# Decode attention over a 1 GB cache: K in 64 KiB rows, one loop per engine, V slots freed by the last product, the gate computed at the start

## The chip, the cores and the metric

One core of one Trainium2 chip runs the kernel alone. The metric is device time in microseconds (us). Each kernel also left one profiled execution, whose span is 1.8 to 2.4 us below its time. Engines: PE does matrix products, DVE is the vector engine, ACT the scalar engine, SP issues DMAs; POOL does almost nothing here (1.4 us busy before). SBUF is the on-chip memory, PSUM the memory into which PE writes. PE's granted clock is the share of its full speed that the profile shows.

## The reference

One query token, 16 heads of 256, a cache of 65536 keys per head, all bf16. The attention output is multiplied by a gate.

```python
xn = _layernorm(x)
q = (xn @ wq).reshape(B, Sq, H, Dh).transpose(0, 2, 1, 3)      # H=16, Dh=256
scores = einsum("bhqd,bhkd->bhqk", q, k_cache) * Dh ** -0.5    # 65536 keys a head
o = einsum("bhqk,bhkd->bhqd", softmax(scores), v_cache)
s = o.transpose(0, 2, 1, 3).reshape(B, Sq, H * Dh) @ wo
g = silu(silu(xn @ w1) @ w2)                                   # the gate
return x + s * g
```

K and V are 537 MB each and are read once. Weights are 10.6 MB.

## The kernel before

A block is 16384 keys: 128 partitions of 128 keys, 8 MiB of K and 8 MiB of V; there are 64. Each block is cut in two tiles of 64 keys per partition, so a partition's row of a tile is 32 KiB. DVE multiplies 13 of every 32 keys by the query in one large product, which ACT sums key by key, and does the other 19 with a fused multiply and sum. Then the block's maximum goes DVE, PE, DVE, PE; ACT takes the exponential; PE multiplies by V one block later.

```python
KT = 64; SUB = 32; ND = 19; TPB = 2
...
    def sp_block(i):                        # K of block i, V of block i - 1, tile by tile
        for t in range(TPB):
            take(sp, kf[t])                 # wait until DVE has freed this K slot
            sp.dma_start(out=Kt[t][:, :], in_=src(Kd, i, t)).then_inc(kl[t], 16)
            take(sp, vf[t])                 # wait until PE has freed this V slot
            sp.dma_start(out=Vt[t][:, :], in_=src(Vd, i - 1, t)).then_inc(vl[t], 16)
...
    def pe_turn():                          # transposes the block's output O
        take(pe, oc)
        ...
                if a == 0 and j == 0:
                    ins.then_inc(vf[1], 1)  # the second V slot is freed here
...
        with nc.Fori(1, NBLK - 1, 1, engines={ET.PE, ET.DVE, ET.Activation, ET.SP}, ...) as i:
            sp_block(i)
            dve_block(i)                    # the query is in SBUF for all heads (qb)
            act_block(i)
            act_keep(i - 1)
            pe_bcast()
            pe_attend()
            pe_rows()
            pe_turn()
```

Block 0 stands ahead of the loop as straight code, the last block behind it. The gate's inner product is done at the start; its last activation is done in the tail.

## Time and profile before

| | before |
|---|---|
| time, median of the first three runs | 2529.64 us (2527.97 to 2530.91) |
| profiled span | 2527.2 us |
| last input packet ends | 2519.7 us |
| tail after it | 7.5 us |
| block period in the middle | 38.87 us |

Two more views matter for what follows. The first gives three stretches after the start. Its columns are the stretch and its length, the busy time and number of instructions of PE, of PE's weight loads, of DVE, ACT and POOL, then PE's granted clock, the busy share of the DMA engines and GB/s:

```profile
60.00:76.00 16.00, 8.61 (x32) 2.96 (x32) 16.00 (x75) 10.20 (x52) 0.00 (x0) 0.87 1.03 442
76.00:84.00 8.00, 3.85 (x10) 1.18 (x11) 8.00 (x40) 4.92 (x25) 0.00 (x0) 0.50 0.98 419
84.00:100.00 16.00, 7.16 (x34) 3.17 (x33) 13.85 (x66) 8.93 (x43) 0.00 (x0) 0.71 0.99 428
```

The DMA share stays at about 1: the start leaves no hole. The second is the end of the chain that ended last (start, duration, what):

```profile
2507.89 3.54 PE ps_a L308 x16
2511.43 1.03 PE ps_t L343 x8
2512.46 3.54 PE ps_a L308 x16
2516.00 1.51 PE ps_ao L679 x8
2517.52 1.03 PE ps_t L343 x8
2518.55 4.64 PE ps_ao L679 x24
```

PE works without a break from the last V products through the projection. The tail is PE's, while the stream is DMA's.

### The profile page before, as it was taken

What the parts mean: (1) busy time and instruction counts of PE and PEld (TensorE: products, weight loads), DVE (VectorE), ACT (ScalarE), POOL (GpSimd) and SP (SyncE); (2) the same over time, 40 slices, a digit from 0 to 9 for tenths busy, and PEclk for the clock granted to TensorE, in tenths of its full rate; (3) what the DMA queues carried; (4) which work ended last, traced back from release to release, by engine and by line L of the source; (5) the groups of instructions that cost most, each with busy time, mean ns of one, the idle gap of its engine ahead of it and who ended that gap; (6) DMA issues with size and microseconds to landing.
All of it is one profiled execution on the core that took longest, in us unless ns stands there. A gap on an engine that the chain in (4) does not pass through costs nothing. (4 is left out here: it accounts for less than half of the span.)

```text
span 2527.2 us, 30558 instructions
## 1 busy us (share of the span) xinstructions
PE 1284.5 (51%) x4945; PEld 483.4 (19%) x4945; DVE 2219.2 (88%) x10276; ACT 1446.6 (57%) x6996; POOL 1.4 (0%) x12
## 2 busy tenths in 40 slices
PE   3554455455544554555455445544554455445547
PEld 1111121111111211111112111111121111111212
DVE  7989898898898988988989889889898898898886
ACT  5656565655565656555656565556565655565553
POOL 0000000000000000000000000000000000000000
PEclk7777777777777777777767776777677767776778
DMA  9999999999999999999999999999999999999998
GB/s 413 432 432 432 432 432 432 432 432 432 432 432 433 432 433 432 432 432 432 432 432 432 432 432 432 432 432 432 432 432 432 432 432 433 432 432 432 432 432 346
DMA packets 40450, 1084.46 MB, mean 429 GB/s; under 512 B 4338, under 2 KB 6516, under 8 KB 6644
## 3 DMA queue, kind: packets, MB, share of 16 engines
q1 hardware_dynamic: 40434, 1084.31, 99.8%
q8 instruction: 4, 0.07, 0.0%
q14 instruction: 10, 0.08, 0.0%
q10 hardware_dynamic: 2, 0.00, 0.0%
HBM read 1084.29 MB, written 0.00 MB: 429 GB/s over the span
## 5 line engine op out<-in xcount | busy, mean ns | idle before, releaser
L262 ACT ACTIVATE junk_a<-prod 128x256 bf16<-128x256 bf16 x3328 | 1330.7, 401 | 746.9 <-ACTq L141 746.9
L308 PE MATMUL psO<-V,PV 128*2 128x512 bf16 x4064 | 1165.2, 458 | 1097.6 <-PEq L141 1097.6
L226 DVE CUSTOM_DVE_ANT_0 junk_d<-K,qcur 128x256 bf16<-128x256 bf16 x4864 | 1698.7, 414 | 0.0
L308 PEld LDWEIGHTS psO<-V,PV 128*2 128x2 bf16 x4064 | 388.4, 97 | 1847.6 <-issue 1520.3
L212 DVE TENSOR_TENSOR prod<-K,qcur 128x3328 bf16<-128x3328 bf16 x256 | 482.9, 1886 | 247.0 <-DVEq L141 247.0
L262 ACT ACTIVATION_READ_ACCUMULATOR junk_a<-prod 128x1 f32 x3328 | 620.0, 186 | 0.0
L226 DVE DVE_READ_ACCUMULATOR2_ANT S<- 128x1 f32 x4864 | 374.2, 77 | 0.0
L295 ACT COPY O<-psO 2x512 f32<-2x512 f32 x64 | 36.8, 574 | 202.4 <-ACTq L141 202.4
L343 PE MATMUL ps_t<-eye,O 2*128 2x1 f32 x520 | 69.6, 251 | 48.4 <-PEq L141 48.4
L343 PEld LDWEIGHTS ps_t<-eye,O 2*128 2x128 f32 x520 | 65.9, 192 | 69.0 <-issue 68.9
L297 ACT COPY hist<-ps_t 128x2 f32 (+1 forms) x65 | 10.4, 160 | 94.9 <-ACTq L141 94.9
L301 PE MATMUL ps_nb<-gmax,ones_row 1*128 1x1 bf16 x65 | 10.3, 159 | 56.1 <-PEq L141 55.6
L191 DVE COPY qcur<-qb 128x256 bf16 (+1 forms) x64 | 14.5, 227 | 25.4 <-issue 15.8
L284 ACT ACTIVATE PV<-S,hist 128x128 bf16<-128x128 f32 (+1 forms) x65 | 26.0, 400 | 2.1
L199 DVE COPY S<-S 128x128 f32<-128x128 f32 (+1 forms) x65 | 14.7, 226 | 9.5
L200 DVE TENSOR_REDUCE rmax<-S 128x1 bf16<-128x128 f32 (+1 forms) x65 | 18.2, 280 | 0.2 <-issue 0.2
L180 DVE TENSOR_REDUCE gmax<-ps_m 1x1 bf16<-1x128 f32 x65 | 17.8, 274 | 0.5 <-DVEq L141 0.5
L301 PEld LDWEIGHTS ps_nb<-gmax,ones_row 1*128 1x128 bf16 x65 | 6.0, 92 | 60.8 <-issue 60.5
L333 PE MATMUL ps_m<-ident,rmax 128*1 128x128 bf16 x65 | 14.3, 220 | 5.7 <-PEq L141 5.7
L488 PE MATMUL ps_a<-xnT,V 128*64 128x1 bf16 x112 | 6.7, 256 | 18.2 <-DMA V<-in_B_w_dram 18.2
L284 ACT ACTIVATION_READ_ACCUMULATOR PV<-S,hist (+1 forms) x65 | 12.1, 186 | 0.0
L488 PEld LDWEIGHTS ps_a<-xnT,V 128*64 128x64 bf16 x112 | 6.6, 210 | 18.7 <-DMA V<-in_B_w_dram 18.7
(65 smaller groups left out, 79.3 us busy)
## 6 DMA issues: line engine op xcount, KB each, us to landing
K<-in_A_k_cache_dram SPq DMA_DIRECT2D x126, 4096.0 KB, 21.3
V<-in_A_v_cache_dram SPq DMA_DIRECT2D x125, 4096.0 KB, 28.7
K<-in_A_k_cache_dram SPq DMA_DIRECT2D x4, 2048.0 KB, 18.5
V<-in_A_v_cache_dram SPq DMA_DIRECT2D x4, 2048.0 KB, 22.9
W<-in_A_v_cache_dram SPq DMA_DIRECT2D x2, 2048.0 KB, 27.3
W<-in_A_wq_dram SPq DMA_DIRECT2D x1, 3072.0 KB, 10.4
K<-in_A_wo_dram SPq DMA_DIRECT2D x3, 896.0 KB, 31.4
V<-in_B_w_dram SPq DMA_DIRECT2D x1, 1568.0 KB, 35.5
```

The lines of the kernel that those rows point to most:

```text
L180: dve.reduce_max(out=gmax[0:1, :], in_=ps_m[0:1, :], axis=AX.X).then_inc(gm, 1)
L191: q_t = own(dve.tensor_copy(out=qcur[:, :], in_=qb[:, sub(q0, Dh)]))
L199: dve.tensor_copy(out=S2[:, c0:c1], in_=S[:, c0:c1]).then_inc(f, 1)
L200: dve.reduce_max(out=rmax[:, :], in_=S[:, c0:c1], axis=AX.X).then_inc(rm, 1)
L212: m = dve.tensor_tensor(out=prod[k % 2][:, :, :], in0=Kv[:, s * SUB + ND : (s + 1) * SUB, :], in1=qcur[:, None, :].to_broadcast([P, NA, Dh ...
L226: ins = dve.tensor_tensor_reduce(out=junk_d[jk][:, :], in0=Kv[:, s * SUB + j, :], in1=qcur[:, :], scale=1.0, scalar=0.0, op0=ALU.mult, op1 ...
L262: ins = act.activation(out=junk_a[jk][:, :], in_=prod[k % 2][:, j, :], func=ACT.Identity, accum_out=S[:, a : a + 1],)
L284: act.activation(out=PV[:, c0:c1], in_=S2[:, c0:c1], func=ACT.Exp, bias=neg, scale=scale, accum_out=hist[:, at(i), 1:2].rearrange("p o s - ...
L295: act.copy(out=O[:, :], in_=po[:, :]).then_inc(oc, 1)
L301: pe.matmul(ps_nb[:, 0:1], lhsT=ones_row[0:1, :], rhs=gmax[0:1, :], start=True, stop=True).then_inc(bm, 1)
L308: ins = pe.matmul(po[:, :], lhsT=PV[:, c0 + c : c0 + c + 2], rhs=T[:, (k0 + c) * Dh : (k0 + c + 2) * Dh], start=(start and c == 0), stop=( ...
L343: ins = pe.matmul(ps_t[:, a : a + 1], lhsT=Ov[:, j, a, :], rhs=eye2[:, j : j + 1], start=(j == 0), stop=(j == 1),)
```

## The change

The intent: fewer, longer DMA packets on a DMA-bound kernel (432 or 433 GB/s in every slice but the first and the last), with the buffers that this needs. K comes in whole blocks of 64 KiB per partition in two 8 MiB slots; V stays in halves of 32 KiB. To make room, the scratch tiles go (DVE and ACT write their throw-away outputs in place), one product tile instead of two, and the weights live in the V slots at first. The query of the next block comes from PE through PSUM. Each engine has its own loop. The gate is finished before the loops and stays in PSUM. The last pieces are ordered anew. Core of the diff, with cuts:

```diff
+    Kt = [pool.tile([P, KB * Dh], bf16, name=f"K{t}") for t in range(2)]   # KB = 128: 64 KiB rows
+    def load_k(i, s):
+        take(sp, kf[s])
+        sp.dma_start(out=Kt[s][:, :], in_=block(Kd, i)).then_inc(kl[s], 16)
...
+    def pe_block(i):
+        take(pe, pv)
+        for t in range(2):
+            take(pe, vl[t], 16)
+            pe_keys(psO, Vt[t], 0, PV, t * VT, VT, t == 0, t == 1, vf[0] if t == 0 else od)
+        pe.matmul(
+            ps_z, lhsT=ident[:, 0:1], rhs=ident[:, 0:1], start=True, stop=True
+        ).then_inc(vf[1], 1)          # second V slot freed right after the products
+        pe_rows(); pe_turn(); pe_bcast()
+        pe_query(i + 1)
...
+        load_rows(wq_t, A_wq, HD, dl["wq"])
+        load_rows(w12_t, B_w1, F, dl["w12"])          # w1, w2 now ahead of K
+        ...
+        for s in range(2):
+            sp.dma_start(out=Kt[s][:, :], in_=block(Kd, s)).then_inc(kl[s], 16)
+        with loop(ET.SP, 0, NBLK - 4, 2) as i:
+            for s in range(2):
+                load_v(i + s)
+                load_k(i + s + 2, s)
...
+        load_keys(Vt[1], VT, Vn, VT, VT + VT // 2, vl[1])        # next-to-last V
+        load_keys(Vt[1], VT, Vn, VT + VT // 2, KB, v2)
+        load_keys(Kt[1], 0, Kl, VT, KB, kh)                      # second half of the last K
...
+        t_g = silu(ps_y, ps_y, prod[...], t)          # the whole gate, before DVE's loop
+        with loop(ET.DVE, 0, NBLK - 2, 2, hint_back_edge=True) as i:
+            for s in range(2):
+                dve_block(s)
+        with loop(ET.Activation, 0, LAST, 1) as i:
+            act_block(i)
```

## The prediction

> **What bounds the kernel now.** I read the page first: busy shares, then the slices, then the queue.
>
> ```profile
> PE 1284.5 (51%) x4945; PEld 483.4 (19%) x4945; DVE 2219.2 (88%) x10276; ACT 1446.6 (57%) x6996; POOL 1.4 (0%) x12
> ...
> DMA  9999999999999999999999999999999999999998
> GB/s 413 432 432 432 432 432 432 432 432 432 432 432 433 432 433 432 432 432 432 432 432 432 432 432 432 432 432 432 432 432 432 432 432 433 432 432 432 432 432 346
> DMA packets 40450, 1084.46 MB, mean 429 GB/s; under 512 B 4338, under 2 KB 6516, under 8 KB 6644
> ...
> q1 hardware_dynamic: 40434, 1084.31, 99.8%
> ```
>
> The reader is to see a flat 432 GB/s from the second slice to the last but one, with all 16 DMA engines busy; only the two ends are lower. No compute engine is full. So the time is start + bytes / rate + tail. Grouped by size, the trace's DMA packet records say the same: 16 packets are in flight in nearly all of 100 to 2400 us, the first data packet starts at 2.02 us and the last input packet ends at 2519.7 us. The tail after it is 2527.2 - 2519.7 = 7.5 us. The timed median, 2529.64, is 2.4 us above the profiled span.
>
> The runner-up is DVE, so I read its waits and one stretch of its timeline in the middle:
>
> ```profile
> DVE prod L212 <- DVEq L141: 247.0, 124, 2.6
> ```
>
> ```profile
> 1215.16 0.23 DVE L199 COPY S<-S 128x128 f32<-128x128 f32 x1
> 1215.31 0.28 DVE L200 TENSOR_REDUCE rmax<-S 128x1 bf16<-128x128 f32 x1
> 1215.84 0.23 DVE L191 COPY qcur<-qb 128x256 bf16 x1 [0.25 <-issue]
> 1217.51 1.89 DVE L212 TENSOR_TENSOR prod<-K,qcur 128x3328 bf16<-128x3328 bf16 x1 [1.44 <-DVEq L141]
> 1237.05 1.89 DVE L212 TENSOR_TENSOR prod<-K,qcur 128x3328 bf16<-128x3328 bf16 x1 [2.53 <-DVEq L141]
> 1245.43 1.89 DVE L212 TENSOR_TENSOR prod<-K,qcur 128x3328 bf16<-128x3328 bf16 x1
> ```
>
> DVE waits twice a block before the big product, 1.44 and 2.53 us here, for K to land: some 4 us of slack in each block. The block period is 38.87 us (K issues at 1215.63 and 2420.47 are 31 blocks apart). The last two rows give a step (product plus 19 fused sums) that nothing delays: 1245.43 - 1237.05 = 8.38 us.
>
> Last, the tail:
>
> ```profile
> 2496.07 0.20 DVE L199 COPY S<-S 128x64 f32<-128x64 f32 x1
> 2496.18 0.21 DVE L200 TENSOR_REDUCE rmax<-S 128x1 bf16<-128x64 f32 x1
> 2496.54 0.22 PE L333 MATMUL ps_m<-ident,rmax 128*1 128x128 bf16 x1 [0.27 <-PEq L141]
> 2496.91 0.28 DVE L180 TENSOR_REDUCE gmax<-ps_m 1x1 bf16<-1x128 f32 x1 [0.51 <-DVEq L141]
> 2497.33 0.16 PE L301 MATMUL ps_nb<-gmax,ones_row 1*128 1x1 bf16 x1 [0.57 <-PEq L141]
> 2523.22 0.61 DVE L688 TENSOR_TENSOR tmp<-ps_ao,g_f 1x448 f32<-1x448 f32 x1 [3.71 <-PE ps_ao L679]
> 2523.86 0.61 DVE L692 TENSOR_TENSOR out_bf<-tmp,x_f 1x448 bf16<-1x448 f32 x1
> 2524.50 0.33 SPq L696 DMA_DIRECT2D out_dram<-out_bf  x1
> ```
>
> The upper five rows are the maximum across partitions: 0.15 us from PE's product to gmax, 0.14 us from gmax to the broadcast. The lower three are the end: from the last projection to the end of the span 4.0 us.
>
> [...] the shortest 16 KiB packet takes 611 ns, the shortest 32 KiB one 1213 ns, so 602 ns for 16 KiB (435 GB/s over 16 engines) and 9 ns fixed. In the steady state a 32 KiB packet costs 1214.1 ns of its engine[...]. [...]
>
> **The change part by part.**
>
> *K in 64 KiB rows.* The bytes stay the same, 1084 MB. Counting K and V rows: before 128 x 256 tiles plus 5 x 128 for tiles cut in halves = 33408 packets. After: K 63 x 128 + 256 = 8320; V 62 x 256 + 1152 for the cut last two blocks = 17024; together 25344. That is 8064 fewer, 504 per engine. [...] **-4.7 us**, all on the bound, because DMA is the bound throughout.
>
> *One K wait per block, private loops, single prod.* The slack of DVE must survive. Per block: 4 steps x 8.38 = 33.5, plus 3 waits for prod at about 0.11 each (a semaphore instruction on DVE's queue is seen every 0.11 us) = 33.9. What was hidden is now exposed, because the query for the next block comes from PE after the broadcast: copy and reduce 0.6, PE row product 0.35, gmax with hop 0.4; then PE's turn of O (1.07) must end before the broadcast 0.2, the query product 0.4 with its register arithmetic some 0.25, the copy out of PSUM 0.35 and its wait 0.1. That is 3.3 to 3.8 us, so 37.2 to 37.7 us against a period of 38.87 - 0.07. DVE keeps 1.1 to 1.6 us. ACT's 13 sums end 1.89 + 5.4 = 7.3 us after the product began, before the next product at 8.4, so one prod is enough. In-place outputs cost nothing by this count and remove waits. **0.**
>
> *V slot freed by its last product.* Before, the second V slot was freed in the turn of O. The V queue was never dry, so **0**.
>
> *Start.* wq stays first (lands at 12.2), but w1 and w2 now go ahead of K (7.7 us by packet times: 8 x (413 + 78 + 476) ns), so K block 0 lands at 19.9 + 19.4 = 39.3 us, and the queue then holds K 1 (to 58.6) and V 0 (to 78). K 2 must be issued by about 77. DVE first does the gate: 112 small products (6.7 us), the activation with a table load, 14 products (5.4), then exp, add, a 2.94 us reciprocal, a product: about 43 us. 43 + 0.4 + 33.9 + 0.4 = 78 for the slot of K 0[...]. That leaves a bubble of 0 to 4 us, I take **+1.5**. Later blocks gain slack.
>
> *Tail.* Counting back from the last packet: wo pieces of 1.25 and 2.5 us, V pieces of 1.27, 1.27, 2.5, 4.9, 4.9, 4.9, wo(0) 6.2, so the second half of the last K lands at -29.7. DVE starts it at about -28.6 (the first half, the first heads' weights of some 3.3 us and gmax end there), two steps 17, maximum and softmax to about -7.6; then PE: 32 products at 0.226 = 7.2 with a turn of 1.07 and a sum 0.4 between, to +1.05; copy of O 0.7, projection of four heads, turn 1.07, to +3.7; DVE 0.4, last projection 0.9, and the end 4.0: **+9.1 us** after the last packet, where it was 7.5. So +1.6. The gate left in PSUM takes 4.5 us of DVE out of the tail, but PE was its bound.
>
> Sum: 2529.6 - 4.7 + 1.5 + 1.6 = **2528 us**.
>
> **The rivals.**
> *DVE becomes the bound.* For: 88% busy, the query chain is new, and only 1.1 to 1.6 us of slack remain; each microsecond over 38.8 costs 62 us. Against: every term above is from the trace and would have to be 40% short. At a period of 39.2 the kernel takes about 2555 us, at 40 it is over 2% slower.
> *A 64 KiB row is cut in two, or reads worse.* Then -4.7 becomes 0 and it takes about 2533; if the 64 KiB pitch costs rate, every 0.1% is 2.5 us.
> *The start stays full and the tail is shorter than I count.* If the gate is done by 40 us[...], 2523.
>
> **Range and chances.** The common cases lie between 2523 and 2533; with some weight on a DVE slightly over its period, 2522 to 2537. Faster by over 2% would need 2479 us[...]: practically excluded. Slower by over 2% (2580) needs DVE at 39.7 us a block: 4%.
>
> **What would show it.** 8064 packets of 64 KiB at about 2419 ns; GB/s a unit or two above 432 in the slices; DVE's wait before the first product of a block down to one of about 1 us; K issues 38.8 us apart. Wrong if the packets are 32 KiB, if DMA slices show gaps early (start) or everywhere with DVE above 95% busy, or if the last packet is much more than 9 us before the end.

Passages are cut from this text because they rested on something that no trace or run here shows. The -4.7 us was 504 packets an engine times a fixed cost per packet that was worked out with a DMA rate no trace shows; with the 9 ns that the text takes from the shortest packets of the trace before (its 435 GB/s is 16 x 16384 B in their 602 ns) it is 504 x 9 = 4.5 us (an estimate), and the sum 2528.2. The +1.5 us held a time from issue to first data that was not shown; the trace after has 0.97 us there (issue at 82.31, first packet at 83.28). The count takes each 64 KiB row as one packet, an assumption then; the trace after has 8064 packets of 65536 bytes. "Practically excluded" had a lower bound beside it: at the page's 432 GB/s the 1084.46 MB take 2510 us (an estimate), also above 2479.

## The result, and the profile after

The changed kernel took 2531.61 us (median of four, 2529.18 to 2531.66), beside 2530.27 for the kernel before. Ratios are the mean time of one kernel's fast runs over that of the other's fast runs of the same rounds, so not quite the ratio of the medians. Here it is 1.0005, 95% interval 0.9987 to 1.0022: the same. Three of the four runs are at 2531.6 and one at 2529.2; more on that below. The kernel before has its own spread, 2527.35 to 2531.34 us over all its runs, for which no cause was looked for.

The page of the changed kernel answers to the lines of the first fence of the prediction:

```profile
PE 1216.1 (48%) x5113; PEld 512.0 (20%) x5113; DVE 2234.7 (88%) x10282; ACT 1443.5 (57%) x6990; POOL 2.5 (0%) x13
DMA  9999999999999999999999999999999999999998
GB/s 415 391 432 432 431 433 441 427 431 439 423 439 431 432 432 431 435 442 424 439 431 426 436 432 431 432 433 435 441 423 439 431 428 434 432 431 432 435 433 336
DMA packets 31348, 1084.47 MB, mean 429 GB/s; under 512 B 3298, under 2 KB 5476, under 8 KB 5860
```

Still DMA-bound (q1's packets take 99.5% of 16 engines' span, 99.8% before), with 9100 packets fewer, but the second slice fell from 432 to 391 GB/s. That slice is 63 us long, so it lost about 6 us. DVE between two blocks in the middle of the kernel:

```profile
1186.14 0.23 DVE L224 COPY S<-S 128x128 f32<-128x128 f32 x1
1186.28 0.28 DVE L225 TENSOR_REDUCE rmax<-S 128x1 bf16<-128x128 f32 x1
1187.12 0.28 DVE L214 TENSOR_REDUCE gmax<-bank 1x1 bf16<-1x128 f32 x1 [0.56 <-DVEq L154]
1189.18 0.42 DVE L231 CAST qcur<-bank 128x256 bf16<-128x256 f32 x1 [1.77 <-DVEq L154]
1191.19 1.89 DVE L240 TENSOR_TENSOR prod<-K,qcur 128x3328 bf16<-128x3328 bf16 x1 [1.58 <-DVEq L154]
1199.57 1.89 DVE L240 TENSOR_TENSOR prod<-K,qcur 128x3328 bf16<-128x3328 bf16 x1
```

The chain of maximum and query is now exposed, 0.56 and 1.77 us, and DVE still waits 1.58 us for K. At first DVE is behind: the first products of the first 14 blocks follow each other 37.23 us apart. Soon after the period is 38.78 us, set by DMA, where it was 38.87.

The loss is at the start. Here are DVE just before its first block, SP's issue of K block 2, and the three stretches again:

```profile
39.50 0.62 DVE L536 TENSOR_TENSOR bank<-bank,prod 1x448 f32<-1x448 f32 x1
47.65 0.42 DVE L231 CAST qcur<-bank 128x256 bf16<-128x256 f32 x1 [7.53 <-DVEq L154]
48.11 1.89 DVE L240 TENSOR_TENSOR prod<-K,qcur 128x3328 bf16<-128x3328 bf16 x1
```

```profile
82.31 0.33 SPq L189 DMA_DIRECT2D K<-in_A_k_cache_dram  x1
```

```profile
60.00:76.00 16.00, 0.00 (x0) 0.00 (x0) 16.00 (x75) 9.83 (x50) 0.00 (x0) 0.50 1.01 436
76.00:84.00 8.00, 1.59 (x8) 1.47 (x8) 6.40 (x37) 5.00 (x25) 0.00 (x0) 0.50 0.51 181
84.00:100.00 16.00, 14.70 (x62) 5.59 (x62) 15.08 (x66) 10.39 (x51) 0.00 (x0) 0.83 0.91 394
```

DVE has finished the gate at 40.1 and starts block 0 at 48.1. The slot of K block 0 comes free too late, and from 76 to 84 us the DMA engines work half the time. In the packet records no data packet is in flight from 79.87 to 83.28 us, 3.4 us; since the packets in flight fall from 16 at 76.5 us to none only at 79.87, 5.7 us of the 16 engines' work are missing. In DVE's sequencer records the 7.8 us lie between the compare-and-branch that enters the loop and the next instruction; ACT, which enters its own loop at 35.6 us, waits 6.9 us at the same place. DVE waited 0.5 us there in the kernel before. That kernel also loaded w1 and w2 behind K and started block 0 at 18.1 us; this order was not tried in the changed kernel.

The last input packet ends at 2521.3 us and the tail is 8.5 us. Its chain, the lines that answer to those of before:

```profile
2513.87 0.36 PE bank L621 x2
2514.23 3.54 PE bank L314 x16
2517.78 1.03 PE bank L342 x8
2518.80 3.54 PE bank L314 x16
2522.35 1.51 PE bank L638 x8
2523.86 1.03 PE bank L342 x8
2524.89 0.87 PE bank L638 x4
```

PE is again busy to the end; the last 24 projections became 4.

So the account in spans is: packets -4.7 (predicted; see below), start +6.3 as the remainder (5.7 of it is the missing work above), together +1.6 on the last packet; tail +1.0; sum +2.6, from 2527.2 to 2529.8.

### The profile page after: what moved, and what is told of

The parts are those of the page before. It is cut to its first block, busy times and chain, and to the rows that moved or that the text cites. A ratio compares the mean times of both kernels' runs of the same rounds, so it can differ in the third digit from the quotient of the medians.

```text
span 2529.8 us, 30572 instructions
## 1 busy us (share of the span) xinstructions
PE 1216.1 (48%) x5113; PEld 512.0 (20%) x5113; DVE 2234.7 (88%) x10282; ACT 1443.5 (57%) x6990; POOL 2.5 (0%) x13
## 3 DMA queue, kind: packets, MB, share of 16 engines
q1 hardware_dynamic: 31330, 1084.31, 99.5%
## 5 line engine op out<-in xcount | busy, mean ns | idle before, releaser
L272 ACT ACTIVATE prod<-prod 128x256 bf16<-128x256 bf16 x3328 | 1330.7, 401 | 781.5 <-ACTq L154 781.5
L251 DVE CUSTOM_DVE_ANT_0 K<-K,qcur 128x256 bf16<-128x256 bf16 x4864 | 1701.2, 422 | 0.0
L314 PE MATMUL bank<-V,PV 128*2 128x512 bf16 x4064 | 1026.6, 417 | 661.3 <-PEq L154 660.8
L314 PEld LDWEIGHTS bank<-V,PV 128*2 128x2 bf16 x4064 | 360.3, 90 | 1313.0 <-issue 894.2
L272 ACT ACTIVATION_READ_ACCUMULATOR prod<-prod 128x1 f32 x3328 | 620.0, 186 | 0.0
L251 DVE DVE_READ_ACCUMULATOR2_ANT S<- 128x1 f32 x4864 | 407.9, 84 | 2.5 <-issue 2.5
L231 DVE CAST qcur<-bank 128x256 bf16<-128x256 f32 x64 | 27.2, 425 | 119.3 <-DVEq L154 119.3
L342 PE MATMUL bank<-eye,O 2*128 2x1 f32 x528 | 121.4, 347 | 1.5 <-PEq L154 1.5
L342 PEld LDWEIGHTS bank<-eye,O 2*128 2x128 f32 x528 | 115.8, 317 | 11.5 <-issue 2.4
L298 ACT COPY O<-bank 2x512 f32<-2x512 f32 x66 | 36.9, 559 | 3.4 <-ACTq L154 3.4
```

Source lines behind the costliest of these rows:

```text
L231: dve.tensor_copy(out=qcur[:, :], in_=ps_q).then_inc(sd, 1)
L251: ins = dve.tensor_tensor_reduce(out=Kv[:, c, :], in0=Kv[:, c, :], in1=qcur[:, :], scale=1.0, scalar=0.0, op0=ALU.mult, op1=ALU.add, accum ...
L272: ins = act.activation(out=prod[:, j, :], in_=prod[:, j, :], func=ACT.Identity, accum_out=S[:, c : c + 1],)
L298: act.copy(out=O[:, :], in_=po).then_inc(oc, 1)
L314: ins = pe.matmul(po, lhsT=W[:, c0 + c : c0 + c + 2], rhs=T[:, (k0 + c) * Dh : (k0 + c + 2) * Dh], start=(start and c == 0), stop=(stop an ...
L342: ins = pe.matmul(ps_t[:, a : a + 1], lhsT=Ov[:, j, a, :], rhs=eye2[:, j : j + 1], start=(j == 0), stop=(j == 1),)
```

## The experiments

**Theory A**: the 64 KiB rows gain what the packet arithmetic says, and a hole in the stream at 77 to 83 us, made by DVE's late start, gives it back. **Theory B**: the start costs nothing in the end, and rate or tail ate the gain. **Theory C**: the 64 KiB rows gain nothing. All kernels gave correct results.

### The gate's activation moved to the tail

```diff
-        t_g = silu(ps_y, ps_y, prod[...], t)            # ahead of DVE's loop
+        t_y = t
...
         weights(N1, NENT, H1, H, (ps_m[:, 0:NL], t15))
+        t_g = silu(g_t, ps_y, res, t_y)                 # beside PE's last products
...                                                      # and the copy of g out of PSUM goes
```

> The gate's activation is taken out of the start and done in the tail, as in the kernel before, so DVE reaches its loop at about 30.5 us instead of 40.1. Theory A (a 5.5 us hole in the DMA stream at 77 to 83 us, caused by DVE starting block 0 at 48.1 instead of 39.3, eats the gain of the 64 KiB rows): block 0 starts at 39 to 40 us, K block 2 is issued at about 74 us, no hole, last packet at about 2515.5, span about 2524, ratio to the kernel before about 0.998. Theory B (the lost time comes from the tail or from a lower DMA rate): no change, span 2527 to 2530.

Measured: 2529.46 us (2527.89 to 2529.78), ratio to before 0.9995 [0.9982, 1.0009]; span 2528.0. DVE still waits 5.8 us at the loop's entry, but now before K has landed, so block 0 starts at 40.8 us:

```profile
35.53 0.42 DVE L231 CAST qcur<-bank 128x256 bf16<-128x256 f32 x1 [5.96 <-DVEq L154]
40.83 1.89 DVE L240 TENSOR_TENSOR prod<-K,qcur 128x3328 bf16<-128x3328 bf16 x1 [4.88 <-DVEq L154]
```

The hole is gone: from 76 to 84 us the DMA moves 436 GB/s. The last packet ends at 2517.7, 3.6 us earlier than in the changed kernel. But the tail grew from 8.5 to 10.3 us. The second of these rows says why (columns as above; PE's granted clock is third from the end):

```profile
2507.00:2510.00 3.00, 1.76 (x10) 0.60 (x7) 0.28 (x1) 0.42 (x2) 0.00 (x0) 1.00 1.02 388
2510.00:2513.00 3.00, 2.66 (x8) 1.01 (x9) 1.78 (x8) 1.29 (x5) 0.00 (x0) 0.60 0.62 231
```

Its mean clock is 0.60; the clock records give 0.5 from 2510.63 to 2514.04 us. PE had idled in three short waits, and the 16 products that followed took 5.29 us where the changed kernel took 3.62. That is 1.7 of the 1.8 us. First this run, then the changed kernel:

```profile
2504.94 3.61 PE L314 MATMUL bank<-K,PV 128*2 128x512 bf16 x16 [1.29 <-DMA K<-in_A_v_cache_dram]
2509.18 0.16 PE L332 MATMUL bank<-gmax,ones_row 1*128 1x1 bf16 x1 [0.57 <-PEq L154]
2510.34 0.36 PE L621 MATMUL bank<-hist,ones_sq 128*128 128x5 f32 x2 [1.00 <-PEq L154]
2510.62 5.29 PE L314 MATMUL bank<-V,PV 128*2 128x512 bf16 x16
```

```profile
2508.47 3.61 PE L314 MATMUL bank<-K,PV 128*2 128x512 bf16 x16 [0.90 <-DMA K<-in_A_v_cache_dram]
2512.72 0.16 PE L332 MATMUL bank<-gmax,ones_row 1*128 1x1 bf16 x1 [0.58 <-PEq L154]
2513.87 0.36 PE L621 MATMUL bank<-hist,ones_sq 128*128 128x5 f32 x2 [1.00 <-PEq L154]
2514.16 3.62 PE L314 MATMUL bank<-V,PV 128*2 128x512 bf16 x16
```

The changed kernel had nearly the same waits and kept its full clock, so the waits alone do not decide it. The five runs fall in two groups, 2527.9 to 2528.1 and 2529.5 to 2529.8, 1.7 us apart, and the profiled one is of the long group: likely the clock fell in three of the five, but no profile of the short group was kept.

Of Theory A the hole and its cause are confirmed, but 3.6 us came back, not 5.7. By 2500 us this kernel's finished packets amount to 5.9 us more work than the changed kernel's, so the rest went between the mean engine and the slowest one. If the bytes still open at 2500 us had gone at 432 GB/s, the last packet would have ended 5.8 us earlier than it did; in the changed kernel it is 3.6. The author's estimate is that the engine that finished last lost only the full stop, 3.4 us, and not the mean 5.7. Counted the same way, the six profiles of the changed kernel and its variants with a full stop give 3.1 to 3.9 us and the five variants without one 5.4 to 6.9, which fits; but the kernel before, without a stop, gives 3.9. Packets carry no engine number here, so none of this split between engines is shown.

### Two blocks ahead of DVE's loop

```diff
+        for s in range(2):
+            dve_block(s)
-        with loop(ET.DVE, 0, NBLK - 2, 2, hint_back_edge=True) as i:
+        with loop(ET.DVE, 2, NBLK - 2, 2, hint_back_edge=True) as i:
```

> The first two K blocks of DVE stand ahead of its loop; the gate stays at the start. It tells whether the 7.8 us between the loop's first branch and its first instruction belong to entering the loop or to anything else at that time. If to entering the loop: block 0 starts at about 40.5 us, the hole at 77 us is gone, and the wait of 3 to 8 us turns up at the third block, near 115 us, where it may open a smaller hole of 0 to 4 us near 155 us; span 2524 to 2528. If it has another cause (gate, semaphores, K landing): block 0 still starts near 48 us and the hole stays.

Measured: 2529.53 us, ratio 0.9998 [0.9983, 1.0013], span 2528.0. With the gate still at the start, DVE goes straight on:

```profile
38.83 0.62 DVE L536 TENSOR_TENSOR bank<-bank,prod 1x448 f32<-1x448 f32 x1
39.37 0.40 DVE L231 CAST qcur<-bank 128x256 bf16<-128x256 f32 x1
40.32 1.89 DVE L240 TENSOR_TENSOR prod<-K,qcur 128x3328 bf16<-128x3328 bf16 x1 [0.55 <-DVEq L154]
```

So the 7.8 us belong to entering the loop there, not to the gate, to a semaphore or to K. The packet records hold one more sign. In all ten profiles where DVE's entry took 5.6 to 7.8 us, at least two 8 KiB packets of the kind that the page calls "instruction" lie inside the wait (in the changed kernel at 40.8, 45.4 and 46.4 us); in the two where it took 0.5 us (this run and the kernel before) none does. That DVE waited for the loop's instructions is a guess from this; no run varied it alone. The hole is gone. The second half of the expectation failed: at 112.4 us, behind straight code, entering the loop costs only 0.5 us; what decides between the two the runs do not settle. The last packet ends at 2519.45, only 1.9 us earlier than in the changed kernel. Three more packets of that kind stand in the records between 105 and 143 us, and the packet of V behind each took 0.66 us longer; that is 2.0 us if one engine carries them, which the records do not tell. In the changed kernel the data packet behind each of its 8 KiB ones between 40 and 2450 us took 0.36 to 0.66 us longer than the median of its size.

### The hint left out

```diff
-        with loop(ET.DVE, 0, NBLK - 2, 2, hint_back_edge=True) as i:
+        with loop(ET.DVE, 0, NBLK - 2, 2) as i:
```

> The prefetch hint for DVE's loop is left out. If the hint causes the 7.8 us at the loop's entry, DVE's block 0 starts near 40.5 us and the hole is gone. If the entry costs it whatever the hint (ACT, without a hint, waits 6.9 us at its own), block 0 still starts at 46 to 48 us, and only the back edge, 0.2 us now, may grow.

One look: 2529.5 us. The hint is an instruction of 0.06 us, BRANCH_PREFETCH_HINT, at 47.44 us in the changed kernel's records. Without the hint DVE still waits 6.2 us at the entry and starts block 0 at 45.5; the jump from the loop's end to its start (the back edge) costs 1.8 us instead of 0.2. The hint is not the cause; it shortens the jump by 1.6 us.

### K in 32 KiB rows again

```diff
-        sp.dma_start(out=Kt[s][:, :], in_=block(Kd, i)).then_inc(kl[s], 16)
+        for c in range(2):
+            w = slice(c * KW // 2, (c + 1) * KW // 2)
+            sp.dma_start(out=Kt[s][:, w], in_=block(Kd, i)[:, w]).then_inc(kl[s], 16)
...                                                      # the first two blocks and DVE's wait likewise
```

> K comes in 32 KiB rows again, two DMAs per block, everything else as in the changed kernel. Theory A (a fixed 9 ns per packet): some 8064 more packets of 32 KiB, block period back from 38.78 to 38.87 us, last packet about 4.7 us later, span about 2534 unless the wait at the loop's entry shrinks with the shorter packets (then down to 2530). Theory C (64 KiB rows gain nothing): period 38.78 as before and span 2529.8.

Measured: 2533.62 us (2532.5 to 2535.25), ratio 1.0016 [1.0002, 1.0030]; span 2531.8. The period is back at 38.85 us. The last packet is only 2.0 us later, but block 0 started at 45.6 us here and the full stop was 0.9 us instead of 3.4, so packet and hole worked against each other. A cleaner pair follows below.

### The second V slot freed in the turn of O

```diff
-        pe.matmul(ps_z, lhsT=ident[:, 0:1], rhs=ident[:, 0:1], ...).then_inc(vf[1], 1)
         pe_rows()
-        pe_turn()
+        pe_turn(free=True)          # its first product does vf[1] += 1
```

> The second V slot is freed in the turn of O again, that is after DVE's block and its maximum, not by the last product. My prediction put this part at 0. Theory A: with K in whole blocks the turn now waits for DVE, so in the first blocks, where DVE is late, the second half of V block 1 is issued at about 121 us while the DMA has run dry at about 112: a hole of about 9 us more, span about 2538. Rival: the V queue is never dry, span 2529.8 as in the changed kernel.

Measured: 2540.82 us (2538.51 to 2542.3), ratio 1.0042 [1.0026, 1.0057]; span 2539.1, 9.3 more than the changed kernel. SP's issues and the two holes:

```profile
95.07 25.86 SPq L194 DMA_DIRECT2D V<-in_A_v_cache_dram  x2
121.18 0.33 SPq L189 DMA_DIRECT2D K<-in_A_k_cache_dram  x1
```

```profile
76.00:84.00 8.00, 1.66 (x8) 1.54 (x9) 6.33 (x37) 4.93 (x24) 0.00 (x0) 0.50 0.49 173
110.00:124.00 14.00, 3.12 (x13) 2.15 (x14) 11.49 (x48) 6.58 (x31) 0.00 (x0) 0.50 0.40 154
```

The two halves of V block 1 were issued at 95 and 121 us, because the turn stands behind DVE's maximum in PE's order. DMA stood still from 115.2 to 121.6 us. Theory A holds (a span of about 2538 us was expected), and in this order of PE's program the part is worth 9 us. One of the four runs, 2538.5, is over 2 us shorter than the rest, as in the changed kernel.

### The changed kernel once more

> The changed kernel once more, unedited, as the neighbour of the next runs on the same chip: span 2527.3 to 2529.8 as in its first runs; the hole at 77 to 83 us again.

Measured: 2531.47 us, ratio 1.0005 [0.9992, 1.0019]; three runs at 2531.5 to 2532.0, two at 2529.0 and 2529.3. The profiled one is of the long group and has the hole. With the four runs above, six runs are long and three short, some 2.5 us apart. In both long profiles block 0 starts at 48.0 to 48.1 us; in the profiles with the same start that gave 2529.5 and 2530.5 us (the hint left out, and the last experiment below) it starts at 45.5, and where the hint was left out 3.3 us of DMA work are missing there instead of 5.7. One 64 KiB packet takes 2.42 us, about this difference; that the loop's entry waits for one packet more or less is the author's guess. No profile of the changed kernel itself fell in the short group, so it was not shown.

### The maximum's products put between the last V's products

On top of gate_tail:

```diff
         for j in range(2):
             pe.wait_ge(va[j], 16)
-            pe_keys(psO, vlast, j * VT // 2, PV2, ...)     # 16 products
-        pe_rows()
-        pe_bcast()
+            # j == 0: 16 products; j == 1: 4 products, pe_rows(), 4 products, pe_bcast(), 8 products
```

> gate_tail, and in the tail the products of the last V's second quarter are cut in three, with the maximum's two small PE products between them, so that the second softmax runs beside those products instead of after them. In gate_tail PE waited 0.57 and 1.00 us there and then ran 16 products in 5.29 us at a granted clock of 0.60 where the changed kernel took 3.62 at 1.00. Theory: the tail after the last packet falls from 10.3 to about 7.5 to 9 us and the span to about 2525 (2526.7 if the clock stays low); ratio to before about 0.9985. Rival (the tail is set by the last landings): no change from gate_tail, 2528.

Measured: 2527.18 us (2527.01 to 2527.26), ratio to before 0.9993 [0.9979, 1.0006]; span 2525.2, tail 7.8. PE's waits of 0.57 and 1.00 us are gone, and the clock stays up where it fell in gate_tail:

```profile
2507.00:2510.00 3.00, 2.29 (x12) 0.97 (x11) 0.81 (x5) 1.23 (x5) 0.00 (x0) 1.00 1.03 392
2510.00:2513.00 3.00, 3.00 (x15) 1.01 (x12) 2.90 (x4) 0.30 (x1) 0.00 (x0) 1.00 0.65 240
```

The gate's 2.94 us reciprocal now lies in the tail (2510.65) beside PE's products and costs nothing visible. Repeated:

> gate_seg once more, unedited, so that it has ten timed rounds against the kernel before: 2527.0 to 2527.3, span 2525.2, no hole. If it is really ahead, each of its runs lies below nearly every run of the kernel before.

2527.27 us (2527.16 to 2527.71), ratio 0.9995 [0.9981, 1.0009]. One of the nine runs of the kernel before beside it, 2527.35, is as short. The ten runs of this version lie between 2527.0 and 2527.7; the 18 runs of the kernel before beside them between 2527.35 and 2531.2, medians 2529.34 and 2528.19. It is ahead of the changed kernel by 4 us of median and of the kernel before by 1 to 2 us, which the intervals do not separate from none.

### 32 KiB rows without a hole

> gate_seg with K in 32 KiB rows, so that the packet size is tried where no hole at the start covers or adds anything. Theory A (9 ns fixed per packet): the last packet 4 to 5 us later than in gate_seg, the block period 38.86 against 38.78 us, time about 2531.7. Theory C (64 KiB rows gain nothing): 2527.2.

Measured: 2532.18 us (2531.97 to 2532.32), ratio 1.0014 [1.0001, 1.0028], period 38.87 us. Against its neighbour (gate_seg_2, on the same chip) it is 4.9 us slower, and the last packet is 4.4 us later. Theory A's packet term is confirmed, Theory C is out.

### The second half of the last K ahead of the next-to-last V's second half

```diff
+        load_keys(Kt[1], 0, Kl, VT, KB, kh)
         take(sp, vf[1])
         load_keys(Vt[1], VT, Vn, VT, VT + VT // 2, vl[1])
         load_keys(Vt[1], VT, Vn, VT + VT // 2, KB, v2)
-        load_keys(Kt[1], 0, Kl, VT, KB, kh)
```

> The second half of the last K goes ahead of the second half of the next-to-last V again, the order of the kernel before. Theory: PE ends the next-to-last block some 6 us later, so the maximum of the first half, and DVE behind it in program order, come later; DVE's last half ends near 2515 instead of 2510.4 and the span grows by 2 to 4 us, to about 2532 or 2533. Rival (the tail is bound by the last V pieces alone): the same span.

Measured: 2535.06 us (2530.54 to 2536.07), ratio 1.0025 [1.0010, 1.0040]. The profiled run is the fastest of the four, so it shows the direction and not the whole size:

```profile
2484.33 8.51 PE L314 MATMUL bank<-V,PV 128*2 128x512 bf16 x32 [5.47 <-PEq L154]
2510.91 0.22 PE L326 MATMUL bank<-ident,rmax 128*1 128x128 bf16 x1 [1.43 <-PEq L154]
```

PE waits 5.5 us for V in the middle of a block, and later 1.4 us for DVE's last maximum, which DVE reaches at 2510.5 us, 3.7 us later than in the run without the hint. Span 2528.8, which is 1.0 above the run without the hint, whose start is the same; the tail is 10.0 us. PE was busy for 55 to 57% of three stretches of 3.41 us in a row here (2504.3 to 2514.6 us), and 16 products still took 3.61 us; in gate_tail, where 16 took 5.29 us at a mean clock of 0.60, it was busy for 54% of the 3.41 us before the fall. What decides it stays open. By the medians it is 3.6 us slower than the changed kernel. The new order helps by 1 to 4 us; more exactly the runs do not say.

## Why the prediction was right or wrong

The time, 2528 predicted and 2531.6 measured, lies in the range, and "the same" was right. That says little of the steps: none of the terms in the sum is over 5 us of 2530. The sum came out 3.6 us low, and the start was its mis-sized term. By its own steps:

- **"K in 64 KiB rows ... -4.7 us"**: right. 8064 packets of 64 KiB (so each such row was one packet), median 2421 ns where 2419 was expected; with and without, 4.9 us in time.
- **DVE "37.2 to 37.7 us"** a block: right at 37.23, seen directly while DVE was behind. DVE did not become the bound. "GB/s a unit or two above 432" is blurred: with longer packets the slices swing from 423 to 442.
- **"V slot freed by its last product ... 0"**: wrong. "The V queue was never dry" was read from the order before, where the turn did not stand behind the whole of DVE's next block. In the new order the old release costs 9 us; the part is needed because of the other parts. It is in the changed kernel, so it is not what the sum missed.
- **Start "+1.5"**: the hole was foreseen in place and cause, but the term was mis-sized. The gate ended earlier than said (40.1, not 43), but entering DVE's loop cost 7.8 us, which no term held. K block 2 was issued at 82.3 us, not 78, and the queue was dry at 79.9. The start took 5.7 us of DMA work (3.6 us came back on the last packet without the hole).
- **Tail "+1.6"**: measured +1.0. The last V products ended 1.05 us after the last packet, as counted. The first 20 projections took 6.3 us, most of it at a granted clock of 0.5 (3.94 us at full clock in the last experiment), but PE waited another 0.90 us for V after them, so this cost nothing.
- **"The gate ... takes 4.5 us of DVE out of the tail, but PE was its bound"**: right, and it should have been read further: those 4.5 us went to the start, where DVE was about to be late. With the gate in the tail again the span is shorter by 1.8 us, and by 4.6 with the tail's waits filled.
- **The rivals**: DVE as the bound and the cut 64 KiB row did not happen. The third, a full start, was reached by the experiments and not by the change, and at 2527.2 us, not 2523. The private loops, the in-place outputs, the single product tile and the query through PSUM were not tried one by one.

## What to carry to other kernels

On a stream that is full from end to end, what a change saves per packet (4.9 us of time here) can be lost at the stream's two ends (5.7 us of DMA work at the start here). Count for each buffer when it comes free against when the queue runs dry, in the first blocks above all, where the consumer starts late (block 0 at 48.1 us here, at 18.1 before). Work moved out of the tail is a gain only if the tail waited for that engine, and a loss if the start does: the gate's end at the start made the span 1.8 us longer here than in gate_tail. A release that was free in one order of an engine's program can sit behind another engine in the next (9 us in vfree_turn).
